# Late banks, fewer places and waiting folds in an attention and Fourier kernel

## The chip, the cores and the metric

The kernel runs on one core of a Trainium2 chip. The metric is device time in microseconds (us) of one execution, as the median of several runs. A core has five engines that matter here: TensorE (PE in the profile, with its weight loads as PEld), VectorE (DVE), ScalarE (ACT), GpSimd (POOL) and SyncE (SP), which issues all transfers of this kernel. TensorE writes its products into eight banks of PSUM, each of 128 partitions by 512 float32 values; ACT and DVE empty them.

## The reference

The output joins two independent results over 2048 tokens of width 448. Everything is float32.

```python
# A: Fourier mixing
a = einsum("bsd,ed->bse", x, dft_hid_re);  b = einsum("bsd,ed->bse", x, dft_hid_im)
y = einsum("ts,bse->bte", dft_seq_re, a) - einsum("ts,bse->bte", dft_seq_im, b)
# B: attention, 16 heads of 28
q, k, v = split(x @ wqkv)
p = softmax(einsum("bhqd,bhkd->bhqk", q, k) * 28 ** -0.5)
out_b = einsum("bhqk,bhkd->bhqd", p, v) reshaped to (1, 2048, 448) @ wo
out = concatenate([y, out_b], axis=-1)
```

## The kernel before

**Products.** To be exact enough, most products use a split: a float32 value becomes a high part and a rest, both in the type float32r, and a product becomes three (high by high, rest by high, high by rest). The products of the softmax weights with the values (P·V) and the *folds* (below) are in float32 itself, with 32 columns of the array for each; four of them run beside each other. In the planner, which is told of next, the float32r products are `mode` 0 and these float32 ones `mode` 1, and a turn from 0 to 1 is charged with PE_TURN, 0.33 us.

**Planner.** No order of instructions is written out. Each piece of work is a `Task` with the engine or engines that can do it, a key (a due time, smaller is earlier), what it depends on, and the places that it needs. `Schedule.run` (L206) goes through planned time: each time an engine falls idle, it takes the ready task of the smallest key whose places are free, and issues it. The order that comes out is fixed when the program is built. Places are tiles in pools (`Slots`): 2 banks for the fill, 6 for attention (L368), `kept` pairs of 128 by 1024 float32 (19, and three more lent by the place of the weights while it is not in use), 4 places for queries `q`, 5 for sums `ou`, 3 for raw weights `wraw`. Places of `q` and `ou` are given in turn, by the smallest key of their users. TensorE keeps to one mode while it has work for it: in mode 1 it takes a mode 0 task only if no mode 1 task is ready (L240); in mode 0 it takes whatever has the smallest key.

**Fill.** Everything but attention on TensorE: projections of queries, keys and values (`project`, `values`), the hidden transform of A (`hidden`, real then imaginary part) and its sequence transform (`sequence`, L649, the largest). Each takes weights or inputs through `Piece`: a transfer into `wraw`, a high part by ACT, a rest by POOL. Its keys run evenly up to T_FILL = 1130.

**Attention.** A unit is a head and a *chunk* of 512 queries, 64 units in all. `TWICE` says how each is done.
- 46 chunks go through `unit_kept` (L796): 16 score products (L809), each copied into half of a `kept` pair by ACT (L416), the running maximum by DVE (L819), then a maximum over all keys by transposes on DVE (L824 to L842); POOL or DVE subtract it (L859), ACT takes the exponential (L863), and two groups of P·V products (`pv_group`, L736) add up the sums in one bank.
- 18 chunks go through `unit_twice` (L744): 16 score products for the maximum alone (L755, DVE L759), the maximum put beside the queries by small transfers, 16 more (L787) that come out with the maximum taken off, the exponential straight from the bank (L791), then the same two P·V groups.

Each kind is a lane that goes through its chunks in order; due times are spread evenly from T_ATT = 34 to T_END = 1100, P_R apart for chunks done twice and P_K apart for kept ones. A chunk's bank of sums, `po`, is copied to an `ou` place by ACT or DVE (`unit_out`). When the four chunks of a head are there (for the last two heads: two chunks), `out_of` (L869) *folds* them: one task of float32 products with `fold` (L878) adds up the four row groups. Small transfers and POOL (L892) then divide by the sums, and the result goes to DRAM.

**End.** When all heads of a chunk are there, the output projection (L988) runs, 16 pieces of eleven products, with keys from T_OUT = 1100.

The queries of a chunk lie in a `q` place from their load (L690, L691, due 12 before the chunk) until the chunk's last score product, in a chunk done twice until the last of L787.

Of the kernel before, what the change touches and what calls it, by code (L numbers as in the profile page):

```python
# [11 lines left out]
F32 = mybir.dt.float32  # L12
F32R = mybir.dt.float32r
# [11 lines left out]
P = 128  # L25
NT = S // P
CH = 512
# [2 lines left out]
VW = 32  # L30
SCALE = DH ** -0.5

NKEPT = 19
DVE_SHIFT = 3
LATE = 110.0
NKEYS = 8
# [27 lines left out]
X_ROWS = 2.0  # L64
AHEAD = 0.15
PE_TURN = 0.33


class Slot:
# [95 lines left out]


class Task:
    __slots__ = ("engs", "key", "emit", "lat", "use", "lock", "left", "then", "mode", "n", "dmas", "own", "since")


class Schedule:
# [8 lines left out]
        self.pools = []  # L180
        self.now = 0.0

    def add(self, engs, key, emit, deps=(), acq=(), use=(), lat=0.15, lock=(), mode=0, dmas=(), own=0.0):
        t = Task()
        t.own = own
        t.engs, t.key, t.emit, t.lat, t.lock, t.mode = engs, key, emit, lat, lock, mode
        t.use, t.then, t.dmas = [*acq, *use], [], dmas
        for s in t.use:
            s.users += 1
            s.key = key if s.key is None else min(key, s.key)  # L190
        t.n = self.n
        deps = [d for d in deps if d is not None]
        t.left = len(deps)
        for d in deps:
            d.then.append(t)
        self.n += 1
        if not deps:
            self.wake(t)
        return t
# [6 lines left out]
    def run(self):  # L206
        events, count = [], 0
        now = self.now = 0.0
        for p in self.pools:
            p.turns.sort(key=lambda s: s.key)  # L210
        idle = {e: False for e in self.ENGINES}
        for n, e in enumerate(self.ENGINES):
            heapq.heappush(events, (FIRST[e], 0, n - 9, "free", (e, None)))
        mode = 0
        done = set()
        landed, flow = [], FLOW_AT
        while True:
            for e in self.ENGINES:
                if not idle[e]:
                    continue  # L220
                aside, pick, first = [], None, None
                if e == "SP" and len(landed) >= LANES and landed[-LANES] > now + 1e-9:
                    heapq.heappush(events, (landed[-LANES], 2, count, "tick", None))
                    continue
                heap = self.ready[e]
                before = now - (AHEAD if e == "PE" else 0.0) + 1e-9
                while heap:
                    item = heapq.heappop(heap)
                    t = item[2]
                    if t.n in done:  # L230
                        continue
                    wants = {}
                    for s in t.use:
                        if s.i is None:
                            wants.setdefault(s.pool, []).append(s)
                    if t.since > before or any(not p.can_take(w, before, now) for p, w in wants.items()) or any(
                            x.lock > now + 1e-9 for x in t.lock):
                        aside.append(item)
                        continue
                    if e == "PE" and mode == 1 and t.mode == 0 and pick is None:  # L240
                        if not any(x[2].mode == 1 and x[2].n not in done for x in heap):
                            pick = t
                            break
                        first = first or item
                        aside.append(item)
                        continue
                    pick = t
                    break
                if pick is None and first:
                    pick = first[2]  # L250
                    aside.remove(first)
                for item in aside:
                    heapq.heappush(heap, item)
                if pick is None:
                    continue
                t = pick
                done.add(t.n)
                for s in t.use:
                    if s.i is None:
                        s.pool.take(s)  # L260
                dur = t.engs[e]
                if e == "PE":
                    if t.mode > mode:
                        dur += PE_TURN
                    mode = t.mode
                lat = t.lat
                if e == "SP":

                    at = now
                    for size, extra in t.dmas:  # L270
                        if len(landed) >= LANES:
                            at = max(at, landed[-LANES])
                        flow = max(flow, at + 0.4) + size / (FLOW if now > T_IN else FLOW_IN)
                        landed.append(max(at + 1.35 + size / 170 + extra + (3.0 if T_IN - 6 < now < 42 else 0.0), flow + 1.1))
                        at += 0.38
                    dur = at - now
                    lat = max(landed[-len(t.dmas):]) - at + 0.1
                t.emit(e)
                count += 1
                idle[e] = False  # L280
                for x in t.lock:
                    x.lock = now + dur + 0.05
                heapq.heappush(events, (now + dur, 0, t.n, "free", (e, t)))
                heapq.heappush(events, (now + dur + t.own, 1, t.n, "own", (e, t)))
                heapq.heappush(events, (now + dur + lat, 1, t.n, "seen", (e, t)))
                if t.lock:
                    heapq.heappush(events, (now + dur + 0.06, 2, t.n, "tick", None))
            if not events:
                break
            now = self.now = events[0][0]  # L290
            while events and events[0][0] <= now + 1e-9:
                _, _, _, what, x = heapq.heappop(events)
                if what == "free":
                    idle[x[0]] = True
                elif what == "own":
                    for n in x[1].then:
                        if x[0] in n.engs and len(n.engs) == 1 and x[0] != "SP":
                            n.left -= 1
                            if n.left == 0:
                                self.wake(n)  # L300
                elif what == "seen":
                    e, t = x
                    for s in t.use:
                        s.users -= 1
                        if s.users == 0:
                            s.home.free.append((s.i, now))
                    for n in t.then:
                        if e in n.engs and len(n.engs) == 1 and e != "SP":
                            continue
                        n.left -= 1  # L310
                        if n.left == 0:
                            self.wake(n, now)
                    heapq.heappush(events, (now + AHEAD, 2, t.n, "tick", None))
        assert count == self.n, (count, self.n, now)
        return now
# [3 lines left out]
def tile_kernel(ctx, tc, xa, wre, wim, wd, xb, wqkv, wo, out):  # L319
# [30 lines left out]
    wlo = new("wlo", [P, 4, P], F32R, 3, True)  # L350
    kt_s = new("k", [P, CH], F32R, NKEYS, True)
    v_s = new("v", [P, NC, 4, VW], F32, 2, True)
    q_s = new("q", [P, CH], F32R, 4, True)
    kept_s = new("kept", [P, 2, CH], F32, NKEPT)
    rm_s = new("rm", [P, CH], F32, 1)
    mb_s = new("mb", [P, CH], F32, 1, True)
    ou_s = new("ou", [P, CH], F32, 5, True)
    sm_s = new("sm", [P, NT], F32, 1)
    mx_s = new("mx", [P, 4, NC], F32, 1)
    nm_s = new("nm", [P, 4], F32, 3)  # L360
# [32 lines left out]
    def pe(key, emit, n=1, d=MS, lat=0.25, **kw):  # L393
        return sch.add({"PE": n * d}, key, emit, lat=lat, **kw)
# [23 lines left out]
            nc.vector.tensor_copy(dst, src)  # L418


    T_ATT, T_END, T_FILL, T_OUT = 34.0, 1100.0, 1130.0, 1100.0
    units = [(h, c) for h in range(H - 2) for c in range(NC)] + [(h, c) for c in LAST for h in (H - 2, H - 1)]
    lane_r = [u for u in units if u[1] in TWICE[u[0]]]
    lane_k = [u for u in units if u[1] not in TWICE[u[0]]]
# [224 lines left out]
    def sequence(part, made):  # L649
        src = wim if part else wre  # L650
        for tt in range(NT):
# [2 lines left out]
            begun = None  # L654
            for q in range(4):
                key = fkey(12, M448)
                w = Piece(lambda tt=tt, q=q: src[tt, :, q * 4:q * 4 + 4, :], key - 12)
                for i in range(12):
                    k, j = divmod(i, 3)

# [83 lines left out]
    def unit_twice(u):  # L744
# [34 lines left out]
        for g in range(NT // GV):  # L779
            tiles, es = [], []  # L780
            for kt in range(GV * g, GV * (g + 1)):
                o = bank_s.slot()
                if kt % 2 == 0:
# [2 lines left out]
                key = t_b + kt * dt  # L786
                m = pe(key, lambda e, o=o, kt=kt: nc.tensor.matmul(  # L787
                    o.t, KT[h][kt // 4].t[:KR + 2, kt % 4 * P:(kt % 4 + 1) * P], q.t[:KR + 2, :], start=True, stop=True),
                    deps=[ld, before.get("rb")], use=[o, p.pair, q, KT[h][kt // 4], po])
                in_line("rb", m)  # L790
                es.append(act(key - 20, lambda o=o, p=p: nc.scalar.activation(p.t, o.t, AF.Exp, scale=SCALE),  # L791
                              deps=[m], use=[o, p.pair]))
# [76 lines left out]
    def out_of(us, rd):  # L869
# [6 lines left out]
        def emit(e):  # L876
            for i, u in enumerate(us):
                nc.tensor.matmul(o.t[i * VW:(i + 1) * VW, :], fold, OU[u].t, start=True, stop=True)  # L878
        m = pe(key, emit, d=0.86, deps=[ou_done[u] for u in us], use=[o, *(OU[u] for u in us)], mode=1)
        a = act(key - 20, lambda: nc.scalar.activation(osb.t[:n * VW], o.t[:n * VW], AF.Copy), deps=[m], use=[o, pair])  # L880

        sm = sm_s.slot()
# [151 lines left out]
```

## Time and profile before

| what | us |
|---|---|
| median of three runs | 1153.86 (1152.3 to 1156.37) |
| the profiled execution | 1153.29 |
| span of its profile | 1151.5 |
| PE, DVE, ACT, POOL busy in the span | 1136.9, 998.5, 1045.6, 926.7 |

The span is from the first to the last instruction that the profile shows. Rows of the table by stretches give, for each stretch of the span, its length and the busy time of each engine with its number of instructions, then TensorE's granted clock as a share of full speed, the share of DMA and the rate in GB/s. Rows of the time line give start, length, engine, line, operation, what is written and read, and how many instructions were merged into the row. Rows of groups give the count, the busy time, the mean of one in nanoseconds, and the idle time of the engine ahead of them with what ended it. Rows of waits give the total, the count and the longest.

### The profile page before, as it was taken

The page shows a single profiled execution, that of the slowest core. Times are in us where ns is not written, and L with a number is a line of the kernel's source. Part 1 is how long each engine was busy: PE and PEld are TensorE (multiplying, and loading weights), DVE is VectorE, ACT ScalarE, POOL GpSimd, SP SyncE. Part 2 cuts the span into 40 slices and gives each one's busy share as a digit, 9 for nine tenths or more (in the row PEclk, how much of TensorE's full clock was granted, in tenths as well). Part 3 has the DMA queues.
Part 4 walks back from the last instruction along what each step waited for, and adds up shares of the span by engine and source line. Part 5 has one row for each costly group of instructions (what it writes and reads, how often), then busy time and mean ns, then how long its engine had stood idle before and what let it go on. Part 6 is the DMA issues. An engine that isn't in the chain of part 4 may idle for free.

```text
span 1151.5 us, 19491 instructions
## 1 busy us (share of the span) xinstructions
PE 1136.9 (99%) x6076; PEld 771.0 (67%) x6076; DVE 998.5 (87%) x1784; ACT 1045.6 (91%) x1783; POOL 926.7 (80%) x549
## 2 busy tenths in 40 slices
PE   8999999999999999999999999999999999999998
PEld 7976666566666766676767666567666766667677
DVE  6599989999999899989989899999998999999812
ACT  5279999999999999999999999999999999999942
POOL 3058887899988889888897999999877998997740
PEclk9999999999999999999999999999999999999999
DMA  8983253222322132232323332222333333323543
GB/s 278 177 196 134 101 186 116 81 81 83 103 71 88 63 109 89 89 96 88 98 89 93 104 97 74 72 89 83 112 99 106 88 114 97 103 66 95 180 144 116
DMA packets 111840, 125.17 MB, mean 109 GB/s; under 512 B 49348, under 2 KB 63316, under 8 KB 111736
## 3 DMA queue, kind: packets, MB, share of 16 engines
q1 hardware_dynamic: 111736, 123.93, 35.9%
q8 instruction: 48, 0.79, 0.3%
q14 instruction: 56, 0.46, 0.1%
HBM read 89.99 MB, written 33.76 MB: 107 GB/s over the span
## 4 chain that ended last, share of the span: by engine, by line
PE 82%; ACT 7%; DVE 6%; issue 2%; POOL 2%; DMA 1%; SPq 0%; DVEq 0%; ACTq 0%; POOLq 0%
PE bank L663 27%; PE bank L736 17%; PE bank L809 14%; PE bank L548 9%; PE bank L787 5%; PE bank L755 5%; PE bank L988 3%; ACT kept L416 3%; DVE rm L819 3%; ACT kept L863 2%; POOL kept L859 2%; PE bank L878 1%; ACT kept L791 1%; DVE mx L759 1%; DMA kept<-wqkv 1%
## 5 line engine op out<-in xcount | busy, mean ns | idle before, releaser
L859 POOL TENSOR_TENSOR kept<-kept,mb 128x1024 f32<-128x1024 f32 x268 | 638.7, 2405 | 86.5 <-ACT mb L844 83.6
L819 DVE TENSOR_TENSOR rm<-bank,rm 128x512 f32<-128x512 f32 x644 | 441.1, 685 | 52.8 <-ACT kept L416 20.0
L416 ACT ACTIVATE kept<-bank 128x512 f32<-128x512 f32 (+1 forms) x696 | 411.3, 659 | 54.1 <-PE bank L809 31.6
L863 ACT ACTIVATE kept<-kept 128x1024 f32<-128x1024 f32 x354 | 385.8, 1135 | 6.1 <-POOL kept L859 3.9
L663 PE MATMUL bank<-big,whi 128*128 128x448 f32 x1024 | 324.2, 368 | 0.3 <-DVE big L644 0.3
L809 PE MATMUL bank<-q,k 84*128 84x512 f32 x736 | 286.2, 414 | 4.6 <-ACT kept L416 2.7
L523 POOL TENSOR_TENSOR wlo<-wraw,whi 128x512 fp32r<-128x512 f32 (+1 forms) x166 | 205.0, 1236 | 85.3 <-ACT whi L517 58.7
L736 PE MATMUL bank<-kept,v 128*32 128x512 f32 x1940 | 241.8, 597 | 0.2
L663 PEld LDWEIGHTS bank<-big,whi 128*128 128x128 f32 x1024 | 193.6, 189 | 31.1 <-issue 4.2
L759 DVE TENSOR_REDUCE mx<-bank 128x1 f32<-128x512 f32 x288 | 194.8, 680 | 8.7 <-PE bank L755 7.7
L809 PEld LDWEIGHTS bank<-q,k 84*128 84x128 f32 x736 | 134.5, 188 | 100.3 <-DVE rm L819 15.3
L663 PE MATMUL bank<-big,wlo 128*128 128x448 f32 x512 | 188.1, 367 | 0.0
L791 ACT ACTIVATE kept<-bank 128x512 f32<-128x512 f32 x262 | 169.6, 670 | 4.9 <-PE bank L787 4.7
L736 PEld LDWEIGHTS bank<-kept,v 128*32 128x32 f32 x1940 | 55.5, 109 | 117.7 <-issue 108.5
L517 ACT ACTIVATE whi<-wraw 128x512 fp32r<-128x512 f32 x167 | 117.8, 706 | 2.1 <-DMA wraw<-wqkv 1.9
L755 PE MATMUL bank<-k,q 84*128 84x512 f32 x288 | 117.3, 410 | 0.5
L787 PE MATMUL bank<-q,k 86*128 86x512 f32 x288 | 115.7, 409 | 0.4
L663 PEld LDWEIGHTS bank<-big,wlo 128*128 128x128 f32 x512 | 96.9, 189 | 14.1 <-issue 0.8
L859 DVE TENSOR_TENSOR kept<-kept,bank 128x1024 f32<-128x1024 f32 x86 | 103.3, 1209 | 3.1 <-ACT mb L844 2.8
L548 PE MATMUL bank<-wd,whi 128*128 128x448 f32 x256 | 79.1, 367 | 0.1
L755 PEld LDWEIGHTS bank<-k,q 84*128 84x128 f32 x288 | 54.0, 188 | 29.2 <-issue 5.9
L787 PEld LDWEIGHTS bank<-q,k 86*128 86x128 f32 x288 | 53.9, 188 | 28.5 <-DVE rm L819 7.3
(83 smaller groups left out, 1103.2 us busy)
## 6 DMA issues: line engine op xcount, KB each, us to landing
wraw<-wre SPq DMA_DIRECT2D x64, 256.0 KB
wraw<-wim SPq DMA_DIRECT2D x64, 256.0 KB
qkd<-wd SPq DMA_DIRECT2D x32, 256.0 KB
wraw<-xa SPq DMA_DIRECT2D x32, 256.0 KB
k<-qkd SPq DMA_DIRECT2D x64, 112.0 KB
q<-qkd SPq DMA_DIRECT2D x64, 112.0 KB
out<-kept SPq DMA_DIRECT2D x32, 224.0 KB
qkd<-kept SPq DMA_DIRECT2D x24, 256.0 KB
```

Source lines behind the costliest of these rows:

```text
L416: nc.scalar.activation(dst, src, AF.Copy)
L523: b = sch.add(e, at, lambda g: eng[g].tensor_tensor(self.lo.t[:, :n], raw.t[:, :n], f32(self.hi.t)[:, :n], op=ALU.subtract), deps=[a], acq ...
L548: nc.tensor.matmul(o.t[:, :cols], w(), x(), start=(i == 0), stop=(i == n - 1))
L663: nc.tensor.matmul(o.t[:, :D], a.t[:, k, :], b[:, q * 4 + k, :], start=(q == 0 and k == 0 and j == 0), stop=(q == 3 and k == 3 and j == 2))
L736: nc.tensor.matmul(o.t[j * VW:(j + 1) * VW, :], VT[h].t[:, kt // 4, j, :], pairs[i // 2].t[:, i % 2, :], start=(kt < 4), stop=(kt >= NT - 4))
L755: m = pe(key, lambda e, o=o, kc=kc, qt=qt: nc.tensor.matmul(o.t, q.t[:KR, qt * P:(qt + 1) * P], KT[h][kc].t[:KR, :], start=True, stop=True ...
L759: ms.append(dve(key - 20, lambda o=o, kc=kc, qt=qt: nc.vector.tensor_reduce(mx.t[:, qt, kc:kc + 1], o.t, axis=AX.X, op=ALU.max), deps=[m], ...
L787: m = pe(key, lambda e, o=o, kt=kt: nc.tensor.matmul(o.t, KT[h][kt // 4].t[:KR + 2, kt % 4 * P:(kt % 4 + 1) * P], q.t[:KR + 2, :], start=T ...
L809: m = pe(key, lambda e, o=o, kt=kt: nc.tensor.matmul(o.t, KT[h][kt // 4].t[:KR, kt % 4 * P:(kt % 4 + 1) * P], q.t[:KR, :], start=True, sto ...
L819: prev = dve(key - 20, lambda o=o: nc.vector.tensor_tensor(rm.t, o.t, rm.t, op=ALU.max), deps=[m, prev], use=[rm, o], lock=[o], own=RAW)
L859: eng[e].tensor_tensor(s.t, s.t, over_pair(pm.t if e == "DVE" else mb.t), op=ALU.add)
L863: es.append(act(key, lambda s=s: nc.scalar.activation(s.t, s.t, AF.Exp, scale=SCALE), 0.96, deps=[sh], use=[s]))
```

## The change

- NKEPT goes from 19 to 20 pairs; `q` from 4 to 3 places; `ou` from 5 to 4 places.
- In `unit_twice` the bank of sums `po` is no longer among what the second score products use, so it is taken by the first P·V group.
- A task can have a `wait`. A fold whose key is under T_END - 30 gets JOIN = 15: while TensorE is in mode 0 and fewer than 15 us of planned time have passed since the fold became ready, it is put aside unless another mode 1 task stands behind it in the list of ready tasks, or nothing else can be issued.
- T_END and T_OUT go from 1100 to 1104.
- In `sequence` the key of each weight load is one unit smaller.

```diff
-NKEPT = 19
+NKEPT = 20
@@
+JOIN = 15.0
@@ Schedule.add
-    def add(self, engs, key, emit, deps=(), acq=(), use=(), lat=0.15, lock=(), mode=0, dmas=(), own=0.0):
+    def add(self, engs, key, emit, deps=(), acq=(), use=(), lat=0.15, lock=(), mode=0, dmas=(), own=0.0, wait=0.0):
         t = Task()
-        t.own = own
+        t.own, t.wait = own, wait
@@ Schedule.run
+                    if e == "PE" and mode == 0 and t.wait and now - t.since < t.wait and not any(
+                            y[2].mode == 1 and y[2].n not in done for y in heap):
+                        first = first or item
+                        aside.append(item)
+                        continue
                     if e == "PE" and mode == 1 and t.mode == 0 and pick is None:
@@ tile_kernel
-    q_s = new("q", [P, CH], F32R, 4, True)
+    q_s = new("q", [P, CH], F32R, 3, True)
-    ou_s = new("ou", [P, CH], F32, 5, True)
+    ou_s = new("ou", [P, CH], F32, 4, True)
-    T_ATT, T_END, T_FILL, T_OUT = 34.0, 1100.0, 1130.0, 1100.0
+    T_ATT, T_END, T_FILL, T_OUT = 34.0, 1104.0, 1130.0, 1104.0
@@ sequence
-                w = Piece(lambda tt=tt, q=q: src[tt, :, q * 4:q * 4 + 4, :], key - 12)
+                w = Piece(lambda tt=tt, q=q: src[tt, :, q * 4:q * 4 + 4, :], key - 13)
@@ unit_twice, second score products
-                    deps=[ld, before.get("rb")], use=[o, p.pair, q, KT[h][kt // 4], po])
+                    deps=[ld, before.get("rb")], use=[o, p.pair, q, KT[h][kt // 4]])
@@ out_of
-        m = pe(key, emit, d=0.86, deps=[ou_done[u] for u in us], use=[o, *(OU[u] for u in us)], mode=1)
+        m = pe(key, emit, d=0.86, deps=[ou_done[u] for u in us], use=[o, *(OU[u] for u in us)], mode=1,
+               wait=JOIN if key < T_END - 30 else 0.0)
```

More of the change, by code (lines that the diff above doesn't have):

```diff
@@ L167 @@
 class Task:
-    __slots__ = ("engs", "key", "emit", "lat", "use", "lock", "left", "then", "mode", "n", "dmas", "own", "since")
+    __slots__ = ("engs", "key", "emit", "lat", "use", "lock", "left", "then", "mode", "n", "dmas", "own", "since", "wait")
 class Schedule:
```

## The prediction

> **What bounds the kernel now.** I read the engine table of the page first, then busy time in six stretches, then single places on the time line. The table:
>
> ```profile
> PE 1136.9 (99%) x6076; PEld 771.0 (67%) x6076; DVE 998.5 (87%) x1784; ACT 1045.6 (91%) x1783; POOL 926.7 (80%) x549
> ```
>
> The six stretches (length, then busy time of PE, PEld, DVE, ACT, POOL):
>
> ```profile
> 0.00:50.00 50.00, 46.42 (x211) 39.54 (x212) 30.30 (x71) 21.90 (x36) 11.00 (x25) 1.00 0.89 239
> 50.00:300.00 250.00, 246.95 (x1258) 158.43 (x1257) 230.00 (x424) 229.95 (x395) 202.19 (x119) 1.00 0.41 120
> 300.00:650.00 350.00, 349.97 (x1935) 237.66 (x1937) 321.14 (x560) 340.59 (x576) 308.15 (x162) 1.00 0.29 90
> 650.00:760.00 110.00, 106.14 (x571) 67.48 (x564) 99.93 (x180) 107.00 (x187) 100.55 (x71) 1.00 0.29 88
> 760.00:1080.00 320.00, 319.88 (x1764) 214.00 (x1763) 293.92 (x509) 311.65 (x526) 279.36 (x149) 1.00 0.32 97
> 1080.00:1151.00 71.00, 67.51 (x353) 53.89 (x351) 23.21 (x44) 34.53 (x69) 25.44 (x26) 1.00 0.47 153
> ```
>
> TensorE never stops from 300 to 650 and from 760 to 1080 (0.03 and 0.12 us idle). It idles 3.6 us at the start, 3.05 us in 50 to 300, 3.86 us in 650 to 760, and after the last product in the tail. ScalarE stands right behind it: 97% busy in 300 to 1080. Its work ends with attention; the tail is TensorE's alone. So the end moves with the length of TensorE's queue, if attention does not end later. What can shorten that queue without dropping a product is idle time or the turns between its two kinds of products (float32r, and the float32 ones of L736 and L878).
>
> **The folds.** A fold on its own (start, length, line, count):
>
> ```profile
> 211.78 0.37 PE L548 MATMUL bank<-wd,whi 128*128 128x448 f32 x1
> 212.08 1.92 PE L736 MATMUL bank<-kept,v 128*32 128x512 f32 x16
> 213.93 0.50 PE L755 MATMUL bank<-k,q 84*128 84x512 f32 x1
> 214.28 0.40 PE L809 MATMUL bank<-q,k 84*128 84x512 f32 x1
> 214.51 0.40 PE L787 MATMUL bank<-q,k 86*128 86x512 f32 x1
> ...
> 214.98 0.36 PE L548 MATMUL bank<-wd,whi 128*128 128x448 f32 x1
> 215.28 1.07 PE L878 MATMUL bank<-ou,fold 128*32 128x512 f32 x8
> 216.27 0.50 PE L755 MATMUL bank<-k,q 84*128 84x512 f32 x1
> 216.61 0.40 PE L809 MATMUL bank<-q,k 84*128 84x512 f32 x1
> ```
>
> and one that happens to stand against a P·V group:
>
> ```profile
> 487.52 0.37 PE L663 MATMUL bank<-big,wlo 128*128 128x448 f32 x1
> 487.83 1.06 PE L878 MATMUL bank<-ou,fold 128*32 128x512 f32 x8
> 488.71 1.90 PE L736 MATMUL bank<-kept,v 128*32 128x512 f32 x16
> 490.54 0.50 PE L755 MATMUL bank<-k,q 84*128 84x512 f32 x1
> ```
>
> From the float32r product before to the one behind, the lone fold takes 216.27 - 214.98 = 1.29 us, and the next step is 0.34 us where 214.51 - 214.28 = 0.23 is usual. The product ahead needs its own 0.20 us anyway (448 columns, where 512 take 0.23): 1.29 + 0.11 - 0.20 = 1.20 us. A P·V group alone spans 213.93 - 211.78 = 2.15 us, group and fold together 490.54 - 487.52 = 3.02 us: beside a group the fold costs 0.87 us. Joining saves 1.20 - 0.87 = 0.33 us.
>
> Of 18 folds, 11 stand alone now; for 10 of them the new wait applies (the last is due after the limit T_END - 30). First and last of the ten are the one at 215.28 and the one at 1069.89; the one at 982.68 has the longest way to its next group:
>
> ```profile
> 982.68 1.07 PE L878 MATMUL bank<-ou,fold 128*32 128x512 f32 x8
> 994.29 1.07 PE L736 MATMUL bank<-kept,v 128*32 128x512 f32 x8
> ...
> 1069.89 1.05 PE L878 MATMUL bank<-ou,fold 128*32 128x512 f32 x4
> ```
>
> 11.6 us is under the 15 us of JOIN, so all ten should join: 10 x 0.33 = **3.3 us** off TensorE. Bounds: nothing (the new order breaks as many accidental neighbours as it makes) to 17 x 0.33 = 5.6. Behind a waiting fold no instruction of an engine is queued, since the wait exists in the planner, which puts other products in its place. What follows a fold late is its ScalarE copy, four small transfers through SP and POOL's L892, all of an earlier head, whose result is wanted only in the output projection.
>
> **Bank of sums taken late (L789).** A twice chunk now holds a bank from its first L787 on; the eighth product comes much later, and only then the first P·V group:
>
> ```profile
> 486.82 0.40 PE L787 MATMUL bank<-q,k 86*128 86x512 f32 x1
> ...
> 509.73 0.40 PE L787 MATMUL bank<-q,k 86*128 86x512 f32 x1
> 511.15 1.92 PE L736 MATMUL bank<-kept,v 128*32 128x512 f32 x16
> ```
>
> That is about 24 us in each chunk's step of 1066 / 19.5 = 54.7 us (T_ATT to T_END over 18 + 1.5): one of six banks is free 44% of the time more. Where it counts is TensorE's waiting ahead of scores:
>
> ```profile
> L809 PE MATMUL bank<-q,k 84*128 84x512 f32 x736 | 286.2, 414 | 4.6 <-ACT kept L416 2.7
> ```
>
> 0.44 x 4.6 = 2.0 us gained. Bounds: the idle time of 50 to 760, 6.9 us, gained at most; as much again lost, if a group of sums finds no bank and keeps four pairs waiting. I take 2.0 as the row that names these waits.
>
> At this place the Trainium skill, "Perfetto Trace Analysis", Optimization Strategy, says that consistent bubbles can mean too little PSUM for the next tile. By that rule all 6.9 us would go, and the sum would come to 1143 us by the profiled execution. The trace disagrees with "consistent": the bubbles are bunched where the fill comes from `hidden`. There POOL sat in three shifts while a `wlo` was due, which no bank cures:
>
> ```profile
> 693.69 7.12 POOL L859 TENSOR_TENSOR kept<-kept,mb 128x1024 f32<-128x1024 f32 x3
> 700.78 0.99 POOL L523 TENSOR_TENSOR wlo<-wraw,whi 128x384 fp32r<-128x384 f32 x1
> ```
>
> **One place fewer for sums (5 to 4).** The places go in turn and a head's fold frees four at once, so four suffice. The fifth served when a chunk of the next head ended before the fold. Now that chunk keeps its bank until the fold: at most once in each of 14 heads, for about half a step of 22.5 us, 154 us against the 18 x 24 = 432 us freed above. That would give back 0.7 of the 2.0 us at most; due times mostly run head by head, so I take 0.2.
>
> **One place fewer for queries (4 to 3).** Loads of queries already go out the moment a place falls free:
>
> ```profile
> 37.99 0.40 PE L809 MATMUL bank<-q,k 84*128 84x512 f32 x1
> ...
> 468.12 0.40 PE L809 MATMUL bank<-q,k 84*128 84x512 f32 x1
> 472.94 0.73 PE L809 MATMUL bank<-q,k 84*128 84x512 f32 x2
> ...
> 534.11 0.40 PE L809 MATMUL bank<-q,k 84*128 84x512 f32 x1
> 540.67 0.73 PE L809 MATMUL bank<-q,k 84*128 84x512 f32 x2
> ```
>
> ```profile
> 534.54 0.34 SPq L690 DMA_DIRECT2D q<-qkd  x1
> ```
>
> At 534.11 a chunk's last product began; as it ended the load started, and the next chunk began 6.6 us after that product. At 468.12 the next chunk's queries had long been there: 4.8 us, the chain of the maximum. With three places two belong to overlapping twice chunks and one to the kept lane, so nearly every change is of the 6.6 us kind: 46 changes x 1.8 us = 83 us of lane time at most. What hides it is the fill, which TensorE takes meanwhile, and the lane's own speed. Its chunks now follow each other every (1058.71 - 37.99) / 45 = 22.7 us (first and last start of a chunk; the last is quoted below), so the 16 products take between 22.7 - 6.6 = 16.1 and 22.7 - 4.8 = 17.9 us; with three places and a step of 22.5 they have 15.9. I cost that at nothing; without the cover it is a rival below. The transfers are the same in number.
>
> **One more pair, later T_END and T_OUT, earlier `wraw`.** The kept lane is behind its due times: its last chunk is due at 34 + 45 x 1066/47.5 = 1043.9 and started here:
>
> ```profile
> 1058.71 0.73 PE L809 MATMUL bank<-q,k 84*128 84x512 f32 x2
> ```
>
> So places and ScalarE hold it, not the key; a pair more of 22 (three are lent) helps the lane catch up, and full TensorE gives nothing for that: 0, with the 2.0 us above as the bound on either side. Four microseconds on T_END let fill go ahead of attention. Attention then ends between 0 and 4 us later; the tail has room (the next part): 0. The `wraw` load of `sequence` has a key one unit smaller; it mostly waits for its place, so SP's order hardly moves: 0.
>
> ```profile
> SPq L516 <- POOL wlo L523: 188.2, 89, 7.7
> ```
>
> **The sum.** The profiled execution took 1153.29 us, span 1151.5. 1153.3 - 3.3 - 2.0 + 0.2 = 1148.2. The median of the three runs is 0.6 above the profiled one: **1149 us**.
>
> **The tail's room.** Last P·V group, last splits of its chunk, last projections (six of 2.25 us; the last four need those splits):
>
> ```profile
> 1104.93 1.92 PE L736 MATMUL bank<-kept,v 128*32 128x512 f32 x16
> ...
> 1133.85 13.66 PE L988 MATMUL bank<-wd,k 128*128 128x448 f32 x66
> ```
>
> ```profile
> 1133.89 1.55 DVE L412 TENSOR_TENSOR k<-kept,k 128x256 fp32r<-128x256 f32 x4
> ```
>
> The splits are done at 1135.4, wanted at 1133.85 + 4.5 = 1138.35: attention may end 2.9 us later before the tail stretches.
>
> **Rivals.** (1) *ScalarE sets the end.* It is 97% busy through attention; then a shorter TensorE queue meets the same end of attention, which T_END pushes 4 us back. The tail chain ends 1151.5 + 4 - 2.9 = 1152.6 in the span, 1154.4 with what lies around, 1155 beside the median: no change. For it: 107.00 of 110 us on ACT where TensorE idles. Against: 0.03 us idle of TensorE in 350. The Trainium skill, "Perfetto Trace Analysis", Identifying the Most-Contended Engine, points the same way: it judges TensorE by its weight loads, 67% here, and takes the engine of highest occupancy, ACT at 91%. The trace bears this out only where fill is dry. (2) *Queries bind the kept lane: slower.* If the lane can't shorten its chunks to 15.9 us, it loses up to 1.8 us at each of 46 changes, 83 us; an eighth of that, 10 us, ends attention 10 us later. Beyond 2.9 us the tail takes it all: 1153.9 + 10 - 2.9 = 1161. It decides from a lag of 2.9 + 5 = 8 us on, the 5 being what folds and bank bring. For: the 16.1 to 17.9 us of today. Against: the lane is 15 us behind at its end after 46 chunks, a third of a microsecond each, so priority over the fill does hold it to its step. (3) *All 6.9 us of idle time go*: 1153.9 - 3.3 - 6.9 = 1144. For: a bank and a pair more. Against: POOL's row above. (4) *The change does not do what it says*: folds stay alone because fresh neighbours replace old ones: 1153.9 - 1.8 = 1152.
>
> **Chances.** Forecast 0.45, (1) 0.20, (2) 0.16, (3) 0.09, (4) 0.10. A measurement tells 0.3%, 3.5 us, from no change: below 1150.4 is faster. Forecast and (3) are faster, (1) and (4) the same, (2) slower; some of the forecast's spread crosses into "the same" and some of (1) into slower: 0.50, 0.31, 0.19. The range takes in (3) and (1), and the nearer part of (2): 1143 to 1158.
>
> **What would show it.** Folds: L878 beside L736, at most two or three alone, turns down by some ten. Bank: the idle column of L809 under 3 us, idle in 650 to 760 under 3 us. Queries: gaps between the kept lane's chunks near 6.6 us everywhere, and L690 ahead of the gap. Wrong if the last L736 starts later than about 1108, if idle shows up in 300 to 650, or if TensorE waits ahead of the last L988.

## The result and the profile after

The changed kernel takes 1146.95 us (median of 6 runs, 1145.6 to 1147.76), the kernel before in the same measurement 1155.38 us (6 runs, 1152.3 to 1158.88): a ratio of 0.9926, 95% interval 0.9907 to 0.9946. That is 8.4 us or 0.74% less; 6.4 us (1155.4 to 1149) had been forecast, counted from the median of this measurement, and 4.9 (1153.9 to 1149) from the one shown before. The profiled execution took 1147.6 us with a span of 1145.8, 5.7 us less than the span of before. The profiled execution of before was one of its shorter ones (1153.29 where the median is 1155.38), that of after one of its longer ones (1147.6 where the median is 1146.95). These two differences, 2.1 and 0.65 us, are the 2.7 us between 8.4 and 5.7.

Lines moved by 6, from the middle of `out_of` on by 7: L809 is now L815, L736 L742, L878 L884. The engine table and two groups of the changed kernel (busy time, mean of one in ns, idle time ahead):

```profile
PE 1131.0 (99%) x6076; PEld 773.7 (68%) x6076; DVE 996.4 (87%) x1779; ACT 1045.7 (91%) x1784; POOL 931.5 (81%) x553
...
L815 PE MATMUL bank<-q,k 84*128 84x512 f32 x736 | 284.2, 410 | 2.6 <-DVE rm L825 1.9
L742 PE MATMUL bank<-kept,v 128*32 128x512 f32 x1988 | 243.4, 599 | 0.2
```

The same work, and TensorE needs 5.9 us less for it; the other engines' busy time moves by 0.1 to 4.8. The six stretches of the changed kernel (length, busy time of PE, PEld, DVE, ACT, POOL, granted clock, share of DMA, GB/s):

```profile
0.00:50.00 50.00, 45.20 (x202) 37.66 (x203) 29.37 (x70) 21.38 (x35) 10.96 (x25) 1.00 0.89 234
50.00:300.00 250.00, 245.65 (x1269) 161.78 (x1268) 233.98 (x428) 231.46 (x399) 197.41 (x119) 1.00 0.41 121
300.00:650.00 350.00, 350.00 (x1943) 236.98 (x1944) 318.43 (x558) 341.73 (x575) 312.42 (x164) 1.00 0.29 90
650.00:760.00 110.00, 108.42 (x577) 72.19 (x579) 98.62 (x178) 106.87 (x187) 102.98 (x71) 0.98 0.29 85
760.00:1080.00 320.00, 319.73 (x1771) 215.71 (x1760) 296.00 (x514) 312.88 (x529) 281.34 (x152) 1.00 0.33 102
1080.00:1151.00 71.00, 61.98 (x328) 49.34 (x326) 20.00 (x35) 31.43 (x63) 26.35 (x26) 0.98 0.42 134
```

TensorE's idle time in 650 to 760 fell from 3.86 to 1.58 us, but that in 0 to 300 rose from 6.6 to 9.15: as a sum of idle time nothing was gained. What is gone are turns. A fold in the changed kernel, and the tail (time line of TensorE: start, length):

```profile
486.77 0.37 PE L669 MATMUL bank<-big,wlo 128*128 128x448 f32 x1
487.07 1.07 PE L884 MATMUL bank<-ou,fold 128*32 128x512 f32 x8
487.96 1.90 PE L742 MATMUL bank<-kept,v 128*32 128x512 f32 x16
489.79 0.96 PE L761 MATMUL bank<-k,q 84*128 84x512 f32 x3
...
1100.09 1.92 PE L742 MATMUL bank<-kept,v 128*32 128x512 f32 x16
1103.37 1.05 PE L884 MATMUL bank<-ou,fold 128*32 128x512 f32 x4
...
1123.83 18.15 PE L995 MATMUL bank<-wd,k 128*128 128x448 f32 x88
```

Only the last fold (1103.37) still stands alone. In the order in which TensorE's products are issued, there are 105 stretches of 32-column products (P·V groups and folds) where the kernel before has 118. Ten of the 13 are the ten folds; three are P·V groups that found another. Attention ends 4.8 us earlier (1104.93 to 1100.09) and the span by as much and 0.9 more.

### The profile page after: what moved, and what is told of

It is laid out like the page before. It is cut to its first block, busy times and chain, and to the rows that moved or that the text cites. A ratio compares the mean times of both kernels' runs of the same rounds, so it can differ in the third digit from the quotient of the medians.

```text
span 1145.8 us, 19477 instructions
## 1 busy us (share of the span) xinstructions
PE 1131.0 (99%) x6076; PEld 773.7 (68%) x6076; DVE 996.4 (87%) x1779; ACT 1045.7 (91%) x1784; POOL 931.5 (81%) x553
## 4 chain that ended last, share of the span: by engine, by line
PE 86%; ACT 5%; DVE 4%; DMA 2%; issue 2%; SPq 0%; DVEq 0%; ACTq 0%; POOLq 0%; POOL 0%
PE bank L669 27%; PE bank L742 19%; PE bank L815 14%; PE bank L554 10%; PE bank L793 6%; PE bank L761 5%; PE bank L995 3%; DVE rm L825 2%; ACT kept L422 2%; DMA kept<-xb 2%; PE bank L884 1%; ACT kept L869 1%; ACT kept L797 1%; ACT whi L523 1%; DVE mx L765 0%
## 5 line engine op out<-in xcount | busy, mean ns | idle before, releaser
L865 POOL TENSOR_TENSOR kept<-kept,mb 128x1024 f32<-128x1024 f32 x273 | 650.7, 2406 | 90.3 <-ACT mb L850 73.9
L422 ACT ACTIVATE kept<-bank 128x512 f32<-128x512 f32 x720 | 427.4, 661 | 54.0 <-PE bank L815 31.3
L869 ACT ACTIVATE kept<-kept 128x1024 f32<-128x1024 f32 x362 | 395.6, 1139 | 5.0 <-POOL kept L865 3.4
L669 PE MATMUL bank<-big,whi 128*128 128x448 f32 x1024 | 327.2, 368 | 0.0
L815 PE MATMUL bank<-q,k 84*128 84x512 f32 x736 | 284.2, 410 | 2.6 <-DVE rm L825 1.9
L529 POOL TENSOR_TENSOR wlo<-wraw,whi 128x512 fp32r<-128x512 f32 (+1 forms) x166 | 205.0, 1237 | 71.7 <-ACT whi L523 50.8
L742 PE MATMUL bank<-kept,v 128*32 128x512 f32 x1988 | 243.4, 599 | 0.2
L669 PEld LDWEIGHTS bank<-big,whi 128*128 128x128 f32 x1024 | 193.8, 189 | 28.1 <-issue 1.7
L815 PEld LDWEIGHTS bank<-q,k 84*128 84x128 f32 x736 | 135.3, 188 | 80.7 <-DVE rm L825 17.2
L669 PE MATMUL bank<-big,wlo 128*128 128x448 f32 x512 | 188.3, 368 | 0.0
L797 ACT ACTIVATE kept<-bank 128x512 f32<-128x512 f32 x270 | 176.8, 679 | 1.7 <-PE bank L793 1.6
L742 PEld LDWEIGHTS bank<-kept,v 128*32 128x32 f32 x1988 | 57.6, 109 | 125.9 <-issue 110.3
L523 ACT ACTIVATE whi<-wraw 128x512 fp32r<-128x512 f32 x167 | 117.8, 708 | 2.6 <-DMA wraw<-wqkv 2.4
L865 DVE TENSOR_TENSOR kept<-kept,bank 128x1024 f32<-128x1024 f32 x89 | 106.9, 1210 | 3.8 <-ACT mb L850 3.6
L669 PEld LDWEIGHTS bank<-big,wlo 128*128 128x128 f32 x512 | 96.9, 189 | 14.3 <-POOL wlo L529 0.8
L761 PEld LDWEIGHTS bank<-k,q 84*128 84x128 f32 x288 | 53.7, 188 | 35.6 <-DVE rm L825 11.5
```

The source lines that it names most:

```text
L422: nc.scalar.activation(dst, src, AF.Copy)
L529: b = sch.add(e, at, lambda g: eng[g].tensor_tensor(self.lo.t[:, :n], raw.t[:, :n], f32(self.hi.t)[:, :n], op=ALU.subtract), deps=[a], acq ...
L669: nc.tensor.matmul(o.t[:, :D], a.t[:, k, :], b[:, q * 4 + k, :], start=(q == 0 and k == 0 and j == 0), stop=(q == 3 and k == 3 and j == 2))
L742: nc.tensor.matmul(o.t[j * VW:(j + 1) * VW, :], VT[h].t[:, kt // 4, j, :], pairs[i // 2].t[:, i % 2, :], start=(kt < 4), stop=(kt >= NT - 4))
L761: m = pe(key, lambda e, o=o, kc=kc, qt=qt: nc.tensor.matmul(o.t, q.t[:KR, qt * P:(qt + 1) * P], KT[h][kc].t[:KR, :], start=True, stop=True ...
L815: m = pe(key, lambda e, o=o, kt=kt: nc.tensor.matmul(o.t, KT[h][kt // 4].t[:KR, kt % 4 * P:(kt % 4 + 1) * P], q.t[:KR, :], start=True, sto ...
```

## The experiments

Twelve kernels ran, in three measurements, each with the kernel before beside it (medians 1155.12, 1156.34 and 1155.33 us; 1155.38 beside the changed kernel). The ratios go by that; a difference in us between kernels of different measurements can be off by about 1 us.

To read them I split each profiled span in the same way. N is the number of 32-column stretches. W is all that TensorE lost by waiting: every step from the start of one product to the start of the next, less the usual step of its kind. Usual is 0.205 us behind a 448-column product, 0.2335 behind a 512-column one, 0.297 into a 32-column stretch, 0.522 out of it and 0.105 more on the step after that, and 0.03 behind a small transposition (0.213 where another follows). A stretch counts from its first start to its last: 1.332 us for 16 products, 2.19 for 24, 3.048 for 32. What is lost at half clock is counted in W.

Then span - 0.33 N - W lies between 1081.9 and 1082.7 us in the kernel before, the changed one and the ten of e1 to e6 and e9 to e12. (e7 and e8 add products.) So turns and waiting together say where every difference between these kernels is. This is an account and not a test of causes: W holds whatever is not usual, and what its closing supports is the price of a turn alone.

"Half" is the time at a granted clock of half, by the trace's clock records, first 40 us and end left out. "ACT idle" is ScalarE's idle time between 60 and 1080 us, gaps over 0.15 us alone; "sums" is what ScalarE waited for P·V products ahead of its copies of sums to `ou`, by the view of its waits.

| kernel | folds wait | bank late | places new | N | W us | half us | ACT idle us | sums us | span us | ratio to before, 95% |
|---|---|---|---|---|---|---|---|---|---|---|
| before | no | no | no | 118 | 30.2 | 0 | 32.9 | 5.3 | 1151.5 | 1 |
| changed | yes | yes | yes | 105 | 28.7 | 3.4 | 28.7 | 4.0 | 1145.8 | 0.9926 (0.9907 to 0.9946) |
| e1 | no | yes | yes | 115 | 29.7 | 0 | 36.1 | 7.4 | 1149.8 | 0.9983 (0.9974 to 0.9993) |
| e2 | yes | no | no | 107 | 44.8 | 13.7 | 43.5 | 9.4 | 1161.9 | 1.0089 (1.0074 to 1.0103) |
| e3 | yes | no | yes | 103 | 52.6 | 20.5 | 51.1 | 23.0 | 1168.8 | 1.0137 (1.0119 to 1.0154) |
| e4 | no | no | yes | 106 | 47.6 | 10.2 | 45.9 | 14.2 | 1165.1 | 1.0101 (1.0086 to 1.0116) |
| e5, e3 with rests first | yes | no | yes | 107 | 39.5 | 10.2 | 44.6 | 15.3 | 1157.0 | 1.0027 (1.0016 to 1.0038) |
| e6, T_END 1100 | yes | yes | yes | 105 | 30.2 | 0 | 33.7 | 6.6 | 1147.0 | 0.9938 (0.9918 to 0.9957) |
| e9 | no | yes | no | 110 | 36.5 | 6.8 | 38.9 | 7.1 | 1155.1 | 1.0027 (1.0017 to 1.0038) |
| e10 | yes | yes | no | 105 | 35.6 | 3.4 | 34.7 | 4.8 | 1152.2 | 0.9984 (0.9974 to 0.9993) |
| e11, e6 with early bank | yes | no | yes | 103 | 54.8 | 17.1 | 53.3 | 24.2 | 1171.2 | 1.0151 (1.0130 to 1.0172) |
| e12, e2 with JOIN 8 | yes | no | no | 111 | 39.4 | 6.8 | 40.2 | 10.1 | 1158.8 | 1.0043 (1.0026 to 1.0060) |

T_END, T_OUT and the key of the weight loads are those of the changed kernel in e1, e3 and e5, those of before in e2, e4, e9, e10 and e12; e6 and e11 have the new key alone.

**e1: no waiting folds.**

```diff
-JOIN = 15.0
+JOIN = 0.0
```

> The changed kernel with JOIN = 0: folds no longer wait. In the order that the planner issues, TensorE now has 115 stretches of products with 32 columns (P.V groups and folds) where the changed kernel has 105 and the kernel before has 118. Theory A (only the number of such stretches counts, 0.33 us each): 10 x 0.33 = 3.3 us slower than the changed kernel, 1 us faster than before, so about 0.996 to 0.999 of before. Rival B (banks and places bring the gain, the waiting nothing): as the changed kernel, 0.993.

1152.99 us, 6.0 over the changed kernel. N rose by 10, W by 1.0: the span grew by 4.0, of which 10 x 0.33 = 3.3 are turns. Theory A holds here; B (waiting brings nothing) falls. In this company the waiting folds are worth 4 to 6 us.

**e2: waiting folds alone.** The hunks of the change for JOIN and `wait`, on the kernel before.

> The kernel before with waiting folds as its only edit: 107 stretches where before has 118. Theory A: 11 x 0.33 = 3.6 us off, ratio 0.997. Rival B: 1.000. If a turn is dearer than the single fold showed (0.5 us and more), 0.995.

1165.79 us: 10.7 us slower than before, which neither theory had. N fell by 11 as foreseen, 3.6 us; W rose by 14.6. So the same edit that saves 6 us in the changed kernel costs 10 in the one before.

**e3: the changed kernel with the bank taken early.**

```diff
-                    deps=[ld, before.get("rb")], use=[o, p.pair, q, KT[h][kt // 4]])
+                    deps=[ld, before.get("rb")], use=[o, p.pair, q, KT[h][kt // 4], po])
```

> The changed kernel with the bank of sums of a chunk done twice taken early again: 103 stretches where the changed kernel has 105. Theory A: 0.7 us less than the changed kernel, ratio to before 0.992. Rival B, the prediction's own step (the late bank brings 2.0 us by shorter idle times): 2.0 us more than the changed kernel, 0.9945, with the idle time in 650 to 760 over 3 us.

1170.82 us: 23.9 us over the changed kernel. Both expectations are far off, A by its sign, B by a factor of twelve. All of it is W (23.9 us more); N is even lower by 2. What such waiting looks like, on TensorE's time line of e3:

```profile
535.83 0.37 PE L669 MATMUL bank<-big,wlo 128*128 128x448 f32 x1
536.03 0.40 PE L815 MATMUL bank<-q,k 84*128 84x512 f32 x1
536.27 0.40 PE L761 MATMUL bank<-k,q 84*128 84x512 f32 x1
537.01 0.49 PE L815 MATMUL bank<-q,k 84*128 84x512 f32 x1 [0.33 <-DVE rm L825]
537.80 0.50 PE L793 MATMUL bank<-q,k 86*128 86x512 f32 x1 [0.30 <-DVE rm L825]
538.40 1.10 PE L815 MATMUL bank<-q,k 84*128 84x512 f32 x2
539.34 0.28 PE L724 MATMUL bank<-ident,nm 128*4 128x128 f32 x1
539.79 0.50 PE L793 MATMUL bank<-q,k 86*128 86x512 f32 x1 [0.18 <-DVE rm L825]
540.59 5.20 PE L742 MATMUL bank<-kept,v 128*32 128x512 f32 x32 [0.29 <-DVE rm L825]
```

From 536.03 on there is no product of the fill (L669), only scores, and each comes 0.6 to 0.8 us after the one before it instead of 0.23: TensorE goes at the pace at which VectorE and ScalarE give banks back. What the next weight tile of the fill waited for stands on the time lines of POOL and ScalarE in e3:

```profile
527.70 14.18 POOL L865 TENSOR_TENSOR kept<-kept,mb 128x1024 f32<-128x1024 f32 x6
541.82 1.31 POOL L529 TENSOR_TENSOR wlo<-wraw,whi 128x512 fp32r<-128x512 f32 x1
540.19 0.61 ACT L523 ACTIVATE whi<-wraw 128x512 fp32r<-128x512 f32 x1
```

Six subtractions stand in a row on POOL ahead of the rest (L529), and theory D, which e5 and e6 test, takes this row for the cause. The rest needs its tile's high part (L523), though, and that was made from 540.19 to 540.80 only: the row held the rest for 1.0 us of its 14. The high part came late on ScalarE, which did copies and exponentials of attention from 526.20 to 540.19 without an idle gap over 0.15 us. This place is no exception: past the first 60 us, a rest starts 0.56 us after its high part ends in e3 and 0.94 in the changed kernel (medians; 0.56 to 1.02 in all twelve of the table). And then the clock halves; the stretches of e3 ahead of, in and behind it:

```profile
537.00:540.40 3.40, 2.62 (x6) 0.96 (x6) 3.21 (x6) 3.40 (x8) 3.40 (x3) 1.00 0.00 0
540.40:543.80 3.40, 3.21 (x16) 0.78 (x20) 3.16 (x6) 3.40 (x6) 2.73 (x2) 0.50 0.38 119
543.80:560.00 16.20, 16.20 (x96) 10.85 (x89) 14.36 (x27) 13.03 (x23) 14.08 (x7) 1.00 0.27 87
```

The P·V stretch of 32 products at 540.59 takes 5.20 us; one of 32 in the changed kernel, at 719.86, takes 3.64. Such times add up to 20.5 us in e3, and 10 us of its W lie in them.

**e4: places alone.** 3 places for queries, 4 for sums, 20 pairs, on the kernel before.

> The kernel before with 3 places for queries, 4 for sums and 20 pairs as its only edits: 106 stretches where before has 118. Theory A: 12 x 0.33 = 4 us off, ratio 0.9965. Rival C (three query places cost the kept lane time that the fill does not hide): 1.000 or more, attention ending over 3 us later. The prediction's step: 1.000.

1167.06 us, 11.9 us slower than before by the medians. N fell by 12 as foreseen (4.0 us), W rose by 17.4. Attention ends later, the last P·V group starting at 1118.54 instead of 1104.93. That is rival C by its result. Its mechanism is not excluded: the kept lane's chunks have gaps of 6.7 us on average (5.4 before) and use 16.4 us instead of 17.3 for their products, so a step takes 23.1 us instead of 22.7, and the last chunk starts at 1077.67 instead of 1058.71. Whether the lane's lag makes the waiting or comes from it is open, and so is which of the three edits does it. Waiting shows in dry stretches like that of e3; on POOL, in one of them:

```profile
687.16 14.17 POOL L859 TENSOR_TENSOR kept<-kept,mb 128x1024 f32<-128x1024 f32 x6
701.30 1.00 POOL L523 TENSOR_TENSOR wlo<-wraw,whi 128x384 fp32r<-128x384 f32 x1
```

with half clock from 698.9 to 702.3. Here too the rest's high part (L517) was late, from 700.23 to 700.89 on ScalarE; the row held the rest for 0.4 us more.

**e5: e3 with the rests first.** In `Piece`, the subtraction on POOL gets a smaller key.

```diff
-            at = key + (0 if early else 1.5)
+            at = key + (0 if early else -10.0)
```

> The kernel of e3_early_bank (the changed kernel with its bank taken early, 1170.8 us) with one further edit: the rests of the fill's weights on POOL (L529) get a key 11.5 smaller, so that fewer subtractions of the maximum (L865) run ahead of them in a row. In the order on POOL there are 6 rows of five and more subtractions where e3 has 11; TensorE has 107 stretches of 32-column products where e3 has 103. Theory D (long rows of subtractions leave the fill without weights, TensorE then steps at the pace of ScalarE and VectorE, and its clock falls to half): half-clock time falls from 20 us to under 7, ratio to before 1.004 or less, 12 us and more under e3. Rival E (the bank itself is what is missing): as e3, 1.013, plus 1 us for four more turns.

1159.21 us, 11.6 under e3, with the bank as early as there. By the time theory D is right for half of the loss. The other half stays: half clock is 10.2 us where under 7 had been expected, and the kernel is still 12 us over the changed one. The mechanism of D is not what the traces show: rests start 0.91 us after their high part here (median), no sooner than in e3. The edit made a new order on all engines (107 stretches, ScalarE idle 44.6 us instead of 51.1), and why that order loses less was not tried.

**e6: T_END and T_OUT at 1100 in the changed kernel.**

> The changed kernel with T_END and T_OUT at 1100 again. Stretches of 32-column products: 105, as in the changed kernel. Rows of five and more subtractions on POOL: 13 where the changed kernel has 8. The prediction's step (the later due times cost and bring nothing): 0.993 of before. Theory D: idle steps and half-clock stretches come back, 8 us and more over the changed kernel, 1.000 or more. The rival of the prediction that T_END ends attention later: 4 us less at most, 0.990.

1149.27 us, ratio 0.9938. The intervals of this and of the changed kernel overlap: the due times are worth 2 us or nothing. Theory D as it was put falls: the trace has 11 rows of five and more subtractions, as many as e3's (8 in the changed kernel's), and yet no half clock at all and a W only 1.5 us over the changed kernel's.

**e7 and e8: turns by themselves.** In both, 32 small products are added to the changed kernel, each overwritten by the next product; the order of all else is the same. e7 uses 32 columns of the array, e8 (second line) all 128.

```diff
+                        if q == 0 and k == 0 and j == 0:
+                            nc.tensor.matmul(o.t[:VW, :VW], fold, ident[:, :VW], start=True, stop=True)
```

```diff
+                            nc.tensor.matmul(o.t[:, :VW], ident, ident[:, :VW], start=True, stop=True)
```

> The changed kernel, its order untouched, with one small float32 product more (128 rows, 32 columns, 32 wide, into the place that the next product overwrites) ahead of each of the 32 output tiles of the sequence transform. Each forces a turn to 32-column products and back. Turn of 0.33 us as read from one fold, and some 0.1 us for the product itself: 32 x 0.43 = 14 us over the changed kernel, 1.004 of before. If a turn costs the 0.65 us that the gain of 8.4 us over 13 turns would need: 24 us, 1.013. If turns cost nothing: 3 us, 0.995.

> As e7, but the small float32 product uses the whole array (128 columns), like the transposes of L724, which in the trace of before stand between float32r products at 0.23 to 0.26 us from start to start in all. If a turn is the change between 32 and 128 columns: 32 x 0.1 to 0.2 = 3 to 6 us over the changed kernel, 0.995 to 0.998 of before, 8 us and more under e7. If it is the change between float32r and float32: as e7.

e7: 1157.34 us (ten executions, one of which took 2824.66; 1157.12 without it), 10.2 to 10.4 over the changed kernel, 0.32 us for a turn with its product. e8: 1152.89 us, 5.9 over it, 0.19 us for a product without one. The 0.33 us read from one fold is thus no underestimate, and 0.65 us for a turn is excluded. The gap between the two, 4.5 us, is smaller than the 8 expected: e8's product is dearer than e7's (each has two weight loads, of 0.19 us in e8 and 0.11 in e7), so the bare turn lies between 0.14 and 0.32 us. From start to start around one of e7's:

```profile
800.91 0.36 PE L671 MATMUL bank<-big,wlo 128*128 128x448 f32 x1
801.20 0.25 PE L670 MATMUL bank<-ident,fold 128*32 128x32 f32 x2
801.38 0.67 PE L671 MATMUL bank<-big,whi 128*128 128x448 f32 x2
801.89 0.37 PE L671 MATMUL bank<-big,wlo 128*128 128x448 f32 x1
```

Product and turn together take 801.38 - 800.91 - 0.205 = 0.27 us there and 0.10 on the next two steps (801.89 - 801.38 - 2 x 0.205). Work was added to TensorE alone, 32 x 0.37 = 11.8 us by these steps, and 10.2 to 10.4 of it came out in the time: TensorE's queue does set the end.

**e9 to e12: is it the bank, or is each new order a new throw?** e9: the bank late as the only edit on the kernel before. e10: that and the waiting folds. e11: e6 with the bank early. e12: e2 with this edit:

```diff
-JOIN = 15.0
+JOIN = 8.0
```

> The kernel before with the late bank as its only edit; 110 stretches of 32-column products where before has 118. Theory L (the bank free for half of a chunk is what keeps TensorE off the slow pace where the fill runs dry; all edits beside it cost without it): no half-clock stretch, ratio 0.997 or less (8 x 0.33 = 2.6 us and some idle time). Rival S (each edit shuffles the order, and what a shuffle brings has nothing to do with the edit): anywhere from 0.990 to 1.015. The prediction's step (2.0 us idle time) with turns: 0.996.

> The kernel before with waiting folds and the late bank, places and due times as before: 105 stretches, as in the changed kernel. Theory L: the 10 us that waiting folds cost alone (e2) are gone, ratio 0.996 or less; as the changed kernel (0.993) if places and due times bring nothing. Rival S: anywhere, 1.005 as likely as 0.995.

> e6 (the changed kernel with T_END 1100, 0.994) with the bank taken early: a second pair of kernels that differ by the bank alone, in other orders than the first (changed kernel and e3). 103 stretches. Theory L: 8 us and more over e6, 1.001 and more, with half-clock stretches of 7 us and more. Rival S: no steady sign, within 5 us of e6 or under it.

> e2 (waiting folds alone, 1.009) with JOIN = 8 instead of 15: 111 stretches where e2 has 107, 2 folds alone in both. If the 10 us of e2 come from the waiting itself: 1.005 to 1.010 again. Rival S: a new order, a new time: 0.995 to 1.003 as likely, and the half-clock time of e2 (13.7 us) need not come again.

e9 was slower, 1.0027: theory L fails alone. e10, 0.9984, is 12.2 us under e2 (1153.6 to 1165.8), from which it differs by the bank alone, though short of the 0.996 expected. e11, 1.0151, is 24.0 us over e6 (1173.3 to 1149.3), the same as between e3 and the changed kernel in other orders. e12 is 1.0043, between the two forecasts: waiting folds on the kernel before cost again, half as much as in e2.

None of the twelve beats the changed kernel.

What follows:
- The late bank is worth 24 us where folds wait and places are few (two pairs: 23.9 and 24.0), 12 us where folds wait alone, and costs 3 us (0.17% to 0.38%) by itself.
- With the late bank the other edits pay: waiting folds take 5.0 us off e9 (to e10) and 6.0 off e1 (to the changed kernel); places, due times and the weight key together take 6.7 us off e10. Without it, waiting folds cost 5.6 to 10.7 us, places 11.9.
- So the gain of 8.4 us has no division into parts of the single edits. By the split, the 5.7 us between the two profiled spans are 13 x 0.33 = 4.3 us of turns and 1.5 us of waiting, 0.1 too much. The other 2.7 us are the difference between profiled executions and medians, of which no trace was kept.
- No kernel was run with an edit that should change nothing but the order. How far a new order alone moves the time is therefore not known; differences of 2 to 3 us (e6, e9) may be no more than that. The 24 us, found in two pairs, are.

**What goes with the waiting.** ScalarE's idle time follows W through the twelve kernels of the table, within 6.4 us (correlation 0.96), while its work hardly differs (1042.3 to 1049.0 us). Ahead of the copies of sums it waits, in e3 and in the changed kernel:

```profile
ACT ou L422 <- PE bank L742: 23.0, 17, 2.5
ACT ou L422 <- PE bank L742: 4.0, 5, 2.4
```

The difference, 19.0 us, stands beside 23.0 us between the two spans; e11 and e6 show 24.2 and 6.6. With the bank early, ScalarE makes 28 to 30 of the 64 copies of sums, with the bank late 21 to 24; VectorE makes the others. So a rival to every story of POOL is that ScalarE, when it idles at such a copy, falls behind with scores and high parts, and TensorE then waits for both. It is not shown: idle time of two engines that wait for each other goes together whichever is first, the kernel before has 29 such copies and waits 5.3 us, and no run moved the copies alone.

## Why the prediction was right

**Right: the bound and the main term.** TensorE's queue set the end, and it was shortened by turns. The ten folds joined, all ten; a lone fold's extra 0.33 us holds as a turn with its small product (0.32 in e7, which also shows that TensorE's queue sets the end). The term was 3.3 us; taken out of the changed kernel the waiting is worth 4.0 us of span (6.0 of medians). Three more turns went, which the prediction had only as accidental neighbours of either sign.

**Wrong: the step "0.44 x 4.6 = 2.0 us gained" for the late bank.** It took the idle time that the trace of before shows ahead of L809 as the thing that a bank can mend. That row did fall, from 4.6 to 2.6 us, exactly as worked out, and nothing was gained by it, since idle time rose elsewhere. Its bounds, 6.9 us on either side, do hold the edit alone (3 us lost, e9), but not its worth beside the other edits, 24 us. The idle time in a trace of before bounds what an edit may remove there, not what it keeps others from adding. The row that the prediction set against a larger gain, three subtractions on POOL ahead of a `wlo`, does not hold either, for the reason found in e3. That rest's high part was made late on ScalarE:

```profile
698.83 0.82 ACT L517 ACTIVATE whi<-wraw 128x512 fp32r<-128x512 f32 x1
```

It ended at 699.65, so POOL held the rest of 700.78 for 1.1 us and not for three subtractions.

**Right in sum, wrong in the parts: places at 0 and -0.2, T_END at 0.** The lane of kept chunks did as worked out: gaps of 6.4 us on average (single ones 2.8 to 10.3) where 6.6 were foreseen (5.4 before), 16.2 us for the products of a chunk where 15.9 were left (17.3 before). Rival 2, that this would bind the lane, did not come in the changed kernel; alone, places cost 12 us, which the prediction had only as this rival. Rival 1 (ScalarE sets the end, time unchanged) did not come as put: ACT's busy time is the same (1045.6, 1045.7) with a span 5.7 us shorter, and attention ended earlier. But that attention ended earlier with the same work on ScalarE goes with less idle time there (28.7 instead of 32.9 us), so ScalarE is not out of the account. The prediction treated the edits as terms of a sum; e2, e3, e4 and e9 show that they are not. That the sum came so near is luck in this: the three edits that each cost time alone (waiting folds 10.7, places 11.9, the late bank 3.3 us) are in the change together, and the prediction had no reason why they need each other.

**The signs it named.** One lone fold (two or three allowed), 13 turns fewer (some ten), 2.6 us ahead of L815 (under 3), 1.6 us idle in 650 to 760 (under 3), last P·V group at 1100.1 (not after 1108), no idle time in 300 to 650: all as stated. That TensorE's clock could fall was not in it.

**Open.** Why the late bank costs 3 us by itself, and how a fold that waits makes the fill run dry with the bank early. e5 recovers half of e3's loss, but by a way that its trace does not show. Whether ScalarE's waits at the copies of sums make the waiting of TensorE was not tried; a run with all these copies on VectorE in e3 would tell.

## What to carry to other kernels

Where a planner orders the work anew, an edit has no price of its own: time the change with each edit taken out and with each edit alone, and expect the two to differ, even in sign. Split the span into counted turns and summed waiting before trusting any story; two numbers closed twelve spans to within 0.8 us. Where filler work keeps the bound engine busy, look at what feeds the filler, and follow it back step by step: a row of long instructions looks like the cause until one asks when the input of the next instruction was there.

## What the hardware showed

TensorE's clock fell to half without a long idle time. In the changed kernel, ahead of and in its one such stretch:

```profile
732.30:735.70 3.40, 2.37 (x12) 0.85 (x15) 3.40 (x6) 3.40 (x7) 3.17 (x3) 1.00 0.00 0
735.70:739.10 3.40, 3.40 (x15) 1.12 (x8) 1.87 (x3) 2.58 (x4) 3.32 (x3) 0.50 0.25 82
```

TensorE shows 70% busy in the 3.4 us ahead, and 77% ahead of the one in e3 that is shown above; its longest single idle time in these two is 0.37 us. The half-clock times last 3.41 us, or 6.83, in all these kernels. The Trainium skill, "TensorE: Matmul & The Clock Gate", "Part 1: The HAM clock gate (the "warmup" mystery)", gives the length of such a window as about 3.4 us, which the trace confirms. It states that the clock falls after an idle window; in these runs it fell after windows that were busy, but thinly used.

The busy share does not tell which windows. The clock stayed full after the first of these (kernel before, 57% busy) and fell after the second (e8, 95% busy), in the third:

```profile
698.60:702.00 3.40, 1.93 (x15) 0.44 (x7) 3.27 (x9) 3.40 (x8) 3.32 (x3) 1.00 0.01 4
660.50:663.90 3.40, 3.23 (x10) 1.51 (x10) 3.25 (x6) 3.40 (x8) 3.24 (x5) 1.00 0.66 205
663.90:667.30 3.40, 3.40 (x10) 2.82 (x10) 2.97 (x5) 2.83 (x5) 3.24 (x3) 0.51 0.61 176
```

What does go with it is the use of the array: count each product with its usual time (0.457 us per 1000 columns; 0.42 us for a P·V or fold product) times the share of the 128 x 128 array that its rows and columns fill. In the fourteen traces, 23 of the 24 falls follow a window with at most 0.37 of this use, the other one with 0.41; of some 4400 other windows at full clock (from 40 to 1130 us) one lies under 0.38. That was counted afterwards and tested by no run. In the changed kernel's one window at half clock lie 1.4 us of W, in the six of e3 10 us, 1.7 each; some of that is waiting that a full clock would have had as well.
